# A fused attention and two-expert kernel: weight loads placed ahead of a round's chunk loads, the fourteenth weight load held back, scaled queries behind x

## The chip, the cores and the metric

The kernel runs on one core of a Trainium2 chip. The metric is the device time of one execution in microseconds (us), as the median of several runs, smaller being better. One further execution was profiled; its trace is what the rows below are read from. The engines are named as in the trace: PE (TensorE, matmuls; PEld its weight loads), DVE (VectorE), ACT (ScalarE), POOL (GpSimd) and SP (SyncE, which here issues nearly all DMAs).

## The reference

```
# decayed linear attention, per head, blocks of 64 tokens, state carried from block to block
intra = ((qb @ kb.T) * Dmask) @ vb               # Dmask[i,j] = lam**(i-j) for i >= j
inter = (qb * lam**(pos+1)) @ kv_state
out   = intra + inter
kv_state = lam**64 * kv_state + (kb * lam**(63-pos)).T @ vb
# first feed-forward, on x = attention output, 1536 tokens x 512
xn = x / sqrt(mean(x*x) + 1e-6) * rms_g
y  = (silu(xn @ w_gate) * (xn @ w_val)) @ w_out        # 512 -> 1536 -> 512
# second feed-forward
out = max(y @ w1, y @ w2, y @ w3) @ w_out2             # 512 -> 768 -> 512
```

q, k, v are float32, 2 batches x 8 heads x 768 tokens x 64. The feed-forward weights are held as 64-bit floats, which the kernel reads as pairs of 32-bit words and turns into float32 itself.

## The kernel before, in words

The 1536 tokens are 12 *chunks* of 128 tokens (two blocks of 64 each). A chunk c needs three *chunk loads*, kn, qn and vn (256 KB each, line L92, called k6, q6, v6 for chunk 6). A *weight unit* is a 128 x 512 float32 tile of one weight matrix, loaded as 512 KB of raw words (tile wraw, line L170). Units are named by matrix and index: g = w_gate, v = w_val, o = w_out, so that g0, v0, g1, v1, g2, o0, o1, v2, g3, v3, o2, o3, g4, v4 are the first fourteen loads in order (in the code they have indices 0 to 13). To keep weight unit v4 and chunk load v4 apart, the units are called "unit v4" and so on. A g or v load is three DMAs (one of 256 KB, two of 128 KB), an o load is one DMA.

Each unit is made by a chain over three engines: ACT L252 and L253 read the raw words, DVE L209, L212, L216 clamp, mask and shift, POOL L219 adds, then ACT L180 and POOL L183 split the float32 result into a high and a low float32r part (wh, wl) for three-pass matmuls on PE.

The program begins with seven hand-ordered *rounds* s = 0 to 6 of attention (a string of letters per round in `orders`, each letter a step with a lag in chunks). In round s PE does in this order: M, the output of chunk s-2 (px, L377); N, the broadcast of the norm of chunk s-3 (pb, L416); C, scores and state of chunk s-1 (sc, L321 and L326); U, the sum of squares (pm, L403); and T, the transposes of chunk s (pk L297, pq L299). After T, ACT copies kT and qT out of PSUM and DVE makes the scaled queries qs (L306) from the same PSUM bank pq. DVE's other steps in a round are x (L418, needs pb), A (L333, needs sc) and the state S (L351); from round 3 on one weight unit is put between them. `loads_at` issues the chunk loads about two chunks ahead, at the start of step T; after the round one raw unit is loaded (`load_to`).

Then comes the first feed-forward (`first_stage`): for token blocks j of 512, gate and value products pg and pv (L490), silu and product, and the output products acc (L480 to L482); the remaining attention rounds are spread between its matmuls at the *gaps* (`gap`, `spread`), and units are made at the same gaps (`third_of_unit`, which calls `begin_unit`). `begin_unit` asks for raw loads up to three units ahead of the one it begins. `lates` becomes non-empty once all attention is done. Raw tiles sit in few buffers: loads with index 10 and up share three of them, so that a load waits until POOL's L219 of the unit three loads before has read its words. SP issues all these DMAs strictly in program order, so a DMA that waits for a buffer holds back every DMA behind it.

Of the kernel before, what the change touches and what calls it, by code (L numbers as in the profile page):

```python
# [9 lines left out]
F32 = mybir.dt.float32  # L10
# [8 lines left out]
P = 128  # L19
# [7 lines left out]
def tile_decay_attention_swiglu_maxout(  # L27
# [136 lines left out]
    def load_to(n):  # L164
        while pos["load"] < min(n, len(raw_list)):
            nm, f = raw_list[pos["load"]]
            more = pos["load"] % 5 > 2 and pos["load"] < 3 * PLAIN - 2
            t = (ld if more else wp).tile([P, KD, 2 * P], I32, tag="raw", name="wraw", bufs=2 if more else 3)
            for to, src in crosswise(t, source[nm](f)) if nm in "gv" else [(t, source[nm](f))]:
                nc.sync.dma_start(out=to, in_=src)  # L170
            raws[nm, f] = t
            pos["load"] += 1
# [58 lines left out]
    def begin_unit():  # L231
        if pos["made"] == len(unit_list):
            return
        key = unit_list[pos["made"]]
        at = group_of[key] % 2
        if first_use[key] <= pos["step"] + 6 and at < len(wpools) and (key is None or room[at]):
            pos["made"] += 1
            if key is None:
                stage1.append((None,) * 5)
                return  # L240
            room[at] -= 1
            held[key] = at
            if key[0][0] == "T":
                stage1.append((key, None if second_sum(key) else words[key[0][1], key[1]], at, None, None))
                return
            load_to(pos["raw"] + (3 if pos["half"] else 1))
            pos["raw"] += 1
            t = raws.pop(key).rearrange("p k (f w) -> p (k f) w", w=2)
            lo, hi = t[:, :, 0], t[:, :, 1]
            W = wp.tile([P, 512], I32, tag="W", name="W", bufs=4)  # L250
            words[key] = W
            nc.scalar.activation(out=W.bitcast(F32), in_=hi.bitcast(F32), func=AF.Abs)  # L252
            nc.scalar.activation(out=lo, in_=lo.bitcast(U32), func=AF.Copy, scale=2.0 ** -29)  # L253
            stage1.append((key, W, at, lo, hi))
# [29 lines left out]
    def decayed_keys(c):  # L284
        keys[c] = kd = att.tile([P, H, D], F32, tag="kd", name="kd", bufs=2)
        r = slice(0, P if c % CPB != CPB - 1 else C)
        nc.gpsimd.tensor_tensor(out=kd[r], in0=qkv[c][0][r], in1=Tm[r, :, C - 1:C].to_broadcast([r.stop, H, D]),
                                op=ALU.mult)

    def turn(c):  # L290
        kn, qn, vn = qkv[c][0], qkv[c][1], qkv[c][2]
        pk = bank("pk")
        pq = bank("pq")
        pkv = pk.rearrange("p (a t) -> p a t", t=P)
        pqv = pq.rearrange("p (a t) -> p a t", t=P)
        for a in range(NP):
            nc.tensor.transpose(pkv[:, a, :], kn[:, 2 * a:2 * a + 2, :].rearrange("p h d -> p (h d)"), ident)  # L297
        for a in range(NP):
            nc.tensor.transpose(pqv[:, a, :], qn[:, 2 * a:2 * a + 2, :].rearrange("p h d -> p (h d)"), ident)  # L299
        kT = att.tile([P, NP, P], F32, tag="kT", name="kT", bufs=1)  # L300
        nc.scalar.copy(out=kT, in_=pkv)
        qT = att.tile([P, NP, P], F32, tag="qT", name="qT", bufs=1)
        nc.scalar.copy(out=qT, in_=pqv)
        qs = att.tile([P, NP, 2, C], F32, tag="qs", name="qs")
        h0 = 0 if c % CPB else 1
        nc.vector.tensor_tensor(  # L306
            out=qs[:, :, h0:], in0=pqv.rearrange("p a (h i) -> p a h i", h=2)[:, :, h0:],
            in1=lami.rearrange("p a (h i) -> p a h i", h=1).to_broadcast([P, NP, 2 - h0, C]), op=ALU.mult)
        if c == 0:
            decayed_keys(0)  # L310
        A = att.tile([P, H, C], F32, tag="A", name="A", bufs=1)
        st[c] = dict(kT=kT, qT=qT, qs=qs, vn=vn, A=A)

    def scores(c):
        d = st[c]
# [14 lines left out]
    def masked(hf):  # L330
        def piece(c):
            d = st[c]
            nc.vector.tensor_tensor(  # L333
                out=d["A"].rearrange("p (a t) i -> p t a i", t=2)[:, hf],
                in0=d["sc"][hf][:, :HF].rearrange("p (a i) -> p a i", i=C),
                in1=Tm.rearrange("p (a t) i -> p t a i", t=2)[:, hf], op=ALU.mult)
            if hf == 0:
                d["S0"] = last_state[0]
                d["S1"] = next_state(c, 0, d["S0"])
        return piece  # L340
# [82 lines left out]
    def rest(c):  # L423
# [5 lines left out]

    named = dict(M=(2, mixed), N=(3, normed), C=(1, scores), a=(1, masked(0)), R=(3, rest),  # L430
                 b=(1, masked(1)), U=(2, summed), V=(1, advance), T=(0, lambda c: (loads_at(c), turn(c))),
                 K=(-1, decayed_keys), k=(0, decayed_keys),
                 w=(3, lambda c: None))
    orders = ["MNCabUVTRK"] * (CPNB + 1) + ["MNCabUVTR", "MNCRabUkVT"] + ["MNCaUkRbVT"] * (NCH - CPNB - 2) + ["MNwRwU", "wwwNwR"]
    attn_q = [(s_, named[ch][1], s_ - named[ch][0]) for s_ in range(NCH + 3) for ch in orders[s_]
              if (ch == "K") <= s_ - named[ch][0] < NCH]
    gaps = [0, 0]
# [1 line left out]
    def attn_step():  # L439
        _, fn, c = attn_q.pop(0)  # L440
        fn(c)
# [514 lines left out]
    with tc.manual_schedule():  # L956
        nc.scalar.dma_start(out=lam8, in_=lam.rearrange("(o h) -> o h", o=1).to_broadcast([P, H]))
        loads_to(0)
        for to, src in crosswise(g_sb, rms_g.rearrange("(a p) -> p a", p=P)):
            nc.scalar.dma_start(out=to, in_=src)  # L960
        make_identity(nc, ident)
        nc.vector.memset(ones, 1.0)
        nc.vector.memset(zeros, 0.0)
        nc.scalar.activation(out=mhalf, in_=zeros[:, 0:1], func=AF.Silu)
        nc.vector.memset(mhalf, -0.5)
        warm = bank("warm")
        for i in range(9):
            nc.tensor.matmul(out=warm[:, 0:P], lhsT=zeros, rhs=zeros, start=True, stop=True)
        nc.vector.tensor_tensor(out=diag, in0=ident[:, :C], in1=ident[:, C:], op=ALU.add)
        for hf in range(2):  # L970
            nc.vector.tensor_copy(out=lamh[64 * hf:64 * hf + 64, :],
                                  in_=lam8.rearrange("p (a t) -> p t a", t=2)[64 * hf:64 * hf + 64, hf, :])
        for a in range(NP):
            nc.vector.tensor_tensor_scan(
                out=lami[:, a, :], data0=lamh[:, a:a + 1].to_broadcast([P, C]), data1=zeros[:, :C],
                initial=1.0, op0=ALU.mult, op1=ALU.add)
        for h in range(H):
            nc.vector.tensor_tensor_scan(
                out=Tm[:, h, :], data0=lam8[:, h:h + 1].to_broadcast([P, C]), data1=diag,
                initial=0.0, op0=ALU.mult, op1=ALU.add)  # L980
        loads_to(1)
        pos["narrow"] = False
        unit_ = None
        for s_ in range(CPNB + 3):
            while attn_q[0][0] == s_:
                fn = attn_q[0][1]
                attn_step()
                if s_ > 2 and fn is named["N"][1]:
                    begin_unit()
                    unit_ = stage1.pop(0)  # L990
                if unit_ and s_ == CPNB + 2:
                    if fn is named["U"][1]:
                        words_of_unit(3, *added_later)
                    elif fn is named["V"][1]:
                        for n in range(3):
                            words_of_unit(n, *unit_, split_add=True)
                        split_unit.append(unit_)
                        stage2.append(unit_[:3])
                elif unit_ and fn is named["b"][1]:
                    words_of_unit(0, *unit_)  # L1000
                elif unit_ and fn is named["U"][1]:
                    words_of_unit(1, *unit_)
                    if stage2:
                        finish_unit(*stage2.pop(0))
                elif unit_ and fn is named["V"][1]:
                    words_of_unit(2, *unit_, split_add=s_ == CPNB + 1)
                    added_later = unit_
                    stage2.append(unit_[:3])
            if s_:
                load_to(pos["load"] + 1)  # L1010
        begin_unit()
        finish = first_stage()
        pos["step"] = len(steps)
        second_stage(finish)
# [31 lines left out]
```

## Time and profile before

| | |
|---|---|
| median of 3 runs | 547.11 us (546.27 to 547.93) |
| the profiled execution's own time | 548.3 us |
| its span, first to last instruction | 546.5 us |
| PE busy | 531.0 us, 97% of the span |
| DVE, POOL, ACT busy | 371.7 us, 300.9 us, 279.7 us |
| mean granted TensorE clock | 0.993 of full speed |

The page divides the span into 40 slices; PE is at 9 tenths or more nearly everywhere except in the first seven slices, the first 95 us, where PE's share goes down to 8 and DMA's is between 7 and 8 tenths in the first five. A busy PE is not PE at its peak, since matmuls are pipelined; what counts in the sections below is where PE's sequence of matmuls stands still.

### The profile page before, as it was taken

The page shows a single profiled execution, that of the slowest core. Times are in us where ns is not written, and L with a number is a line of the kernel's source. Part 1 is how long each engine was busy: PE and PEld are TensorE (multiplying, and loading weights), DVE is VectorE, ACT ScalarE, POOL GpSimd, SP SyncE. Part 2 cuts the span into 40 slices and gives each one's busy share as a digit, 9 for nine tenths or more (in the row PEclk, how much of TensorE's full clock was granted, in tenths as well). Part 3 has the DMA queues.
Part 4 walks back from the last instruction along what each step waited for, and adds up shares of the span by engine and source line. Part 5 has one row for each costly group of instructions (what it writes and reads, how often), then busy time and mean ns, then how long its engine had stood idle before and what let it go on. Part 6 is the DMA issues. An engine that isn't in the chain of part 4 may idle for free.

```text
span 546.5 us, 9743 instructions
## 1 busy us (share of the span) xinstructions
PE 531.0 (97%) x3728; PEld 438.2 (80%) x3728; DVE 371.7 (68%) x680; ACT 279.7 (51%) x541; POOL 300.9 (55%) x247
## 2 busy tenths in 40 slices
PE   8998988999999999999999999999999999999997
PEld 7776756788888888888888888888888888888886
DVE  4776775545967676768677575887777477684464
ACT  3667674336264565464447426646466755651120
POOL 2485886241436486385556636886287544962050
PEclk9979999999999999999999999999999999999999
DMA  8888817000202132131221221121123222200015
GB/s 191 203 209 235 213 40 186 9 2 0 78 0 63 54 116 68 49 115 40 77 88 65 78 57 60 40 77 40 38 79 114 85 75 75 82 34 0 0 44 188
DMA packets 65598, 44.67 MB, mean 82 GB/s; under 512 B 40080, under 2 KB 61840, under 8 KB 65552
## 3 DMA queue, kind: packets, MB, share of 16 engines
q1 hardware_dynamic: 64848, 44.05, 28.4%
q8 instruction: 29, 0.48, 0.4%
q14 instruction: 17, 0.14, 0.1%
q10 hardware_dynamic: 704, 0.01, 0.1%
HBM read 40.90 MB, written 3.15 MB: 81 GB/s over the span
## 4 chain that ended last, share of the span: by engine, by line
PE 85%; DMA 4%; issue 2%; POOL 2%; SPq 2%; DVE 2%; ACT 2%; POOLq 0%; ACTq 0%; DVEq 0%
PE p L683 34%; PE acc L874 9%; PE r L683 8%; PE acc L480 6%; PE acc L482 6%; PE acc L481 6%; PE pv L490 5%; PE q L683 4%; PE pg L490 4%; DMA wraw<-in_moe_w_val_dram 3%; SPq L170 2%; PE px L377 1%; POOL W L219 1%; DMA qn<-in_q_dram 1%; PE sc L326 1%
## 5 line engine op out<-in xcount | busy, mean ns | idle before, releaser
L183 POOL TENSOR_TENSOR wl<-W,wh 128x512 fp32r<-128x512 f32 x77 | 100.7, 1309 | 60.5 <-ACT wh L180 60.5
L219 POOL TENSOR_TENSOR W<-W,wraw 128x512 int32<-128x512 int32 x60 | 80.6, 1343 | 71.9 <-DVE W L216 61.7
L180 ACT CAST wh<-W 128x512 fp32r<-128x512 f32 x77 | 47.8, 621 | 80.3 <-POOL W L219 78.8
L501 POOL TENSOR_TENSOR hl<-sg,hh 128x512 fp32r<-128x512 f32 x36 | 47.2, 1311 | 34.3 <-ACT hh L500 34.3
L683 PE MATMUL p<-xl,wh 128*128 128x512 f32 x148 | 57.6, 389 | 0.0
L683 PE MATMUL p<-xh,wl 128*128 128x512 f32 x148 | 57.6, 389 | 0.0
L683 PE MATMUL p<-xh,wh 128*128 128x512 f32 x148 | 57.6, 389 | 0.0
L480 PE MATMUL acc<-hh,wh 128*128 128x512 f32 x144 | 56.8, 394 | 0.7 <-DVE W L216 0.7
L481 PE MATMUL acc<-hl,wh 128*128 128x512 f32 x144 | 56.2, 390 | 0.0
L482 PE MATMUL acc<-hh,wl 128*128 128x512 f32 x144 | 56.1, 390 | 0.0
L252 ACT ACTIVATE W<-wraw 128x512 f32<-128x512 f32 x60 | 40.3, 672 | 9.9 <-DMA wraw<-in_moe_w_dram 4.4
L838 DVE TENSOR_TENSOR acc_sb<-acc,acc_sb 128x512 f32<-128x512 f32 x46 | 31.7, 690 | 19.5 <-PE acc L482 18.3
L209 DVE TENSOR_SCALAR mid<-W 128x512 f32<-128x512 f32 x58 | 39.8, 686 | 6.1 <-ACT W L252 6.1
L212 DVE TENSOR_SCALAR mid<-mid 128x512 int32<-128x512 int32 x58 | 40.3, 694 | 0.8
L216 DVE SCALAR_TENSOR_TENSOR W<-wraw,mid 128x512 int32<-128x512 int32 x58 | 39.5, 682 | 1.1
L253 ACT ACTIVATE wraw<-wraw 128x512 int32<-128x512 uint32 x60 | 39.9, 665 | 0.0
L738 ACT COPY c<-p 128x512 f32<-128x512 f32 x34 | 20.0, 587 | 38.3 <-PE p L683 38.3
L501 POOL TENSOR_TENSOR hl<-m,hh 128x512 fp32r<-128x512 f32 x18 | 24.2, 1350 | 23.0 <-ACT hh L500 23.0
L683 PE MATMUL p<-yl,wh 128*128 128x512 f32 x90 | 35.0, 389 | 0.0
L683 PE MATMUL p<-yh,wh 128*128 128x512 f32 x90 | 35.0, 389 | 0.0
L683 PE MATMUL p<-yh,wl 128*128 128x512 f32 x90 | 35.0, 389 | 0.0
L500 ACT CAST hh<-sg 128x512 fp32r<-128x512 f32 x36 | 22.3, 619 | 22.8 <-DVE sg L624 16.8
(176 smaller groups left out, 1322.9 us busy)
## 6 DMA issues: line engine op xcount, KB each, us to landing
wraw<-in_moe_w_out_dram SPq DMA_DIRECT2D x18, 512.0 KB, 3.4
wraw<-in_moe_w_dram SPq DMA_DIRECT2D x18, 512.0 KB, 3.5
kn<-in_k_dram SPq DMA_DIRECT2D x12, 256.0 KB, 4.3
qn<-in_q_dram SPq DMA_DIRECT2D x12, 256.0 KB, 4.7
vn<-in_v_dram SPq DMA_DIRECT2D x12, 256.0 KB, 4.9
wraw<-in_moe_w_gate_dram SPq DMA_DIRECT2D x12, 256.0 KB, 3.0
wraw<-in_moe_w_gate_dram SPq DMA_DIRECT2D x24, 128.0 KB, 3.3
wraw<-in_moe_w_val_dram SPq DMA_DIRECT2D x12, 256.0 KB, 3.0
```

Source lines behind the costliest of these rows:

```text
L180: nc.scalar.copy(out=wh, in_=W.bitcast(F32))
L183: nc.gpsimd.tensor_tensor(out=wl, in0=W.bitcast(F32), in1=wh.bitcast(F32), op=ALU.subtract)
L212: nc.vector.tensor_scalar(out=mid[key], in0=mid[key], scalar1=0x07FFFFFF, scalar2=3, op0=ALU.bitwise_and, op1=ALU.logical_shift_left)
L219: nc.gpsimd.tensor_tensor(out=W, in0=W, in1=lo, op=ALU.add)
L252: nc.scalar.activation(out=W.bitcast(F32), in_=hi.bitcast(F32), func=AF.Abs)
L480: nc.tensor.matmul(out=out, lhsT=wh, rhs=xh_, start=first, stop=False)
L481: nc.tensor.matmul(out=out, lhsT=wh, rhs=xl_, start=False, stop=False)
L482: nc.tensor.matmul(out=out, lhsT=wl, rhs=xh_, start=False, stop=last)
L490: nc.tensor.matmul(out=ps, lhsT=w[:, kk * P:(kk + 1) * P], rhs=x[:, kk, :], start=n == 0, stop=n == len(todo) - 1)
L501: nc.gpsimd.tensor_tensor(out=dst_l, in0=src, in1=dst_h.bitcast(F32), op=ALU.subtract)
L683: nc.tensor.matmul(out=ps, lhsT=w[:, ks], rhs=r[:, o + k, :], start=first and k == 0 and n == 0, stop=k == 1 and n == 2, skip_group_check= ...
L874: nc.tensor.matmul(out=acc[:, cs], lhsT=x[:, ts], rhs=w[:, cs], start=n == 0, stop=n == len(todo) - 1)
```

## The change

Three edits. First, in rounds 1 to 6 the raw weight load of the round is issued just ahead of step T, which starts the round's chunk loads, where it used to come after the round. Second, in the first feed-forward, as long as attention is not done, `begin_unit` asks for at most thirteen raw loads; unit v4 (index 13) is so asked for only after attention is done. Third, in rounds 0 to 5 step T (now the letter t) leaves out the scaled queries, and a new step Q makes them in the next round, behind N, whose last DVE instruction is x; the tile A is allocated where it is first written.

```diff
-            load_to(pos["raw"] + (3 if pos["half"] else 1))
+            load_to(min(pos["raw"] + 3, 3 * PLAIN + 1) if pos["half"] and not lates else pos["raw"] + (3 if lates else 1))
...
-    def turn(c):
+    def turn(c, scaled=True):
...
+        st[c] = dict(kT=kT, qT=qT, pq=pqv, vn=vn)
+        if scaled:
+            scaled_queries(c)
+        if c == 0:
+            decayed_keys(0)
+
+    def scaled_queries(c):
+        pqv = st[c].pop("pq")
         qs = att.tile([P, NP, 2, C], F32, tag="qs", name="qs")
...
-        if c == 0:
-            decayed_keys(0)
-        A = att.tile([P, H, C], F32, tag="A", name="A", bufs=1)
-        st[c] = dict(kT=kT, qT=qT, qs=qs, vn=vn, A=A)
+        st[c]["qs"] = qs
...
+            if hf == 0:
+                d["A"] = att.tile([P, H, C], F32, tag="A", name="A", bufs=1)
...
+                 t=(0, lambda c: (loads_at(c), turn(c, False))), Q=(1, scaled_queries),
...
-    orders = ["MNCabUVTRK"] * (CPNB + 1) + ["MNCabUVTR", "MNCRabUkVT"] + ["MNCaUkRbVT"] * (NCH - CPNB - 2) + ["MNwRwU", "wwwNwR"]
+    orders = ["MNQCabUVtRK"] * (CPNB + 1) + ["MNQCabUVtR", "MNQCRabUkVT"] + ["MNCaUkRbVT"] * (NCH - CPNB - 2) + ["MNwRwU", "wwwNwR"]
...
+                if s_ and fn in (named["t"][1], named["T"][1]):
+                    load_to(pos["load"] + 1)
                 attn_step()
...
-            if s_:
-                load_to(pos["load"] + 1)
```

The first place is SP's queue around the end of the rounds. The piece is a difference: the rows above it end with unit v1, and vn, kn, qn in its first lines are v5, k6 and q6.

```order
 L170 DMA wraw<-in_moe_w_val_dram 64x2x256 x2
 L92 DMA vn<-in_v_dram 128x8x64
+L92 DMA kn<-in_k_dram 128x8x64
+L92 DMA qn<-in_q_dram 128x8x64
 L170 DMA wraw<-in_moe_w_gate_dram 128x2x256
 L170 DMA wraw<-in_moe_w_gate_dram 64x2x256 x2
+L92 DMA vn<-in_v_dram 128x8x64
+L170 DMA wraw<-in_moe_w_out_dram 128x1024
 L92 DMA kn<-in_k_dram 128x8x64
 L92 DMA qn<-in_q_dram 128x8x64
 L92 DMA vn<-in_v_dram 128x8x64
```

Before, unit v1 stood behind v5, k6 and q6 and was followed by v6; now it stands ahead of these three, unit g2 ahead of v6, and unit o0 ahead of the loads of chunk 7. In every round from 1 on, the three chunk loads and the unit have changed places in this way.

The second place is SP's queue at the last two chunks. In this piece of the difference the gate rows are unit g4, the removed rows are unit v4, and kn and qn are those of chunk 10.

```order
 L170 DMA wraw<-in_moe_w_gate_dram 128x2x256
 L170 DMA wraw<-in_moe_w_gate_dram 64x2x256 x2
-L170 DMA wraw<-in_moe_w_val_dram 128x2x256
-L170 DMA wraw<-in_moe_w_val_dram 64x2x256 x2
 L92 DMA kn<-in_k_dram 128x8x64
 L92 DMA qn<-in_q_dram 128x8x64
```

Unit v4's three DMAs now follow the six loads of chunks 10 and 11.

The third place is DVE in rounds 4 to 5: before, and then of the changed kernel (its line numbers are shifted; L314 is qs, L425 is x).

```order
L216 SCALAR_TENSOR_TENSOR W<-wraw,mid 128x512
L306 TENSOR_TENSOR qs<-pq,lami 128x512
L418 TENSOR_TENSOR x<-x,pb 128x512
L333 TENSOR_TENSOR A<-sc_680,Tm 128x4x64
```

The changed kernel has at the same place, after the same row of W:

```order
L425 TENSOR_TENSOR x<-x,pb 128x512
L314 TENSOR_TENSOR qs<-pq,lami 128x512
```

The two change places in rounds 2 to 5's boundaries (four times); on PE, ACT and POOL every instruction stands where it stood.

## Rows read from the trace of the kernel before

**Rows 1.** Windows by stage: busy time by engine, granted clock, DMA share, GB/s.
```profile
0.00:39.30 39.30, 34.51 (x793) 30.74 (x794) 27.45 (x95) 23.02 (x56) 19.12 (x24) 0.91 0.85 202
39.30:92.30 53.00, 45.76 (x661) 34.73 (x660) 37.02 (x85) 35.87 (x77) 39.95 (x36) 1.00 0.63 164
...
120.00:527.00 407.00, 407.00 (x1797) 337.18 (x1797) 284.19 (x456) 209.81 (x380) 229.31 (x177) 1.00 0.19 59
```

**Rows 2.** Waits of PE, 14 to 100 us: total us, times, longest.
```profile
PE pk L297 <- DMA kn<-in_k_dram: 1.5, 1, 1.5
...
PE pm L403 <- DVE zeros L394: 1.2, 3, 0.6
PE px L377 <- ACT sg L621: 1.1, 1, 1.1
PE pb L416 <- DVE mid L212: 1.1, 1, 1.1
```

**Rows 3.** Timeline of PE at the transposes of chunk 10: start, us, idle before.
```profile
87.62 0.39 PE L490 MATMUL pg<-xh,wl 128*128 128x512 f32 x1
89.50 0.63 PE L297 MATMUL pk<-ident,kn 128*128 128x128 f32 x4 [1.49 <-DMA kn<-in_k_dram]
90.45 0.41 PE L299 MATMUL pq<-ident,qn 128*128 128x128 f32 x2 [0.33 <-DMA qn<-in_q_dram]
```

**Rows 4.** Timeline of SP, 64 to 92 us: units g4 and v4, then k10.
```profile
69.09 1.69 SPq L170 DMA_DIRECT2D wraw<-in_moe_w_gate_dram  x3
84.16 1.67 SPq L170 DMA_DIRECT2D wraw<-in_moe_w_val_dram  x3
85.92 0.54 SPq L92 DMA_DIRECT2D kn<-in_k_dram  x1
```

**Rows 5.** The chain that ended last, 60 to 120 us: start, us, what.
```profile
82.82 1.32 POOL W L219
```

**Rows 6.** Timeline of SP, 26 to 47 us: q6, then unit v1.
```profile
29.75 1.79 SPq L92 DMA_DIRECT2D qn<-in_q_dram  x1
31.59 4.04 SPq L170 DMA_DIRECT2D wraw<-in_moe_w_val_dram  x3
```

**Rows 7.** The chain, 0 to 60 us: last DMA of unit v1, issue to landing.
```profile
35.03 4.89 DMA wraw<-in_moe_w_val_dram
```

**Rows 8.** DMA issues at 29.9 us (q6 alone): count, size, us from issue to landing.
```profile
qn<-in_q_dram SPq DMA_DIRECT2D x1, 256.0 KB, 6.4
```

**Rows 9.** Timeline of PE where the rounds end and the first feed-forward begins.
```profile
39.02 0.60 PE L299 MATMUL pq<-ident,qn 128*128 128x128 f32 x4
39.38 0.48 PE L490 MATMUL pg<-xh,wh 128*128 128x512 f32 x1
```

**Rows 10.** Waits of ACT, 14 to 52 us: total us, times, longest.
```profile
ACT W L252 <- DMA wraw<-in_moe_w_val_dram: 3.2, 2, 2.2
...
ACT W L252 <- DMA wraw<-in_moe_w_gate_dram: 1.6, 2, 1.2
ACT W L252 <- DMA wraw<-in_moe_w_out_dram: 0.7, 1, 0.7
```

**Rows 11.** Waits of DVE, 0 to 39.5 us: total us, times, longest.
```profile
DVE A L333 <- PE sc L326: 4.4, 4, 1.6
...
DVE x L418 <- PE pb L416: 1.2, 2, 0.8
...
DVE qs L306 <- ACT qT L303: 0.3, 1, 0.3
```

**Rows 12.** Windows of 5 us, columns as in rows 1.
```profile
25.00:30.00 5.00, 3.66 (x135) 2.94 (x133) 4.04 (x13) 4.02 (x12) 4.02 (x5) 1.00 0.80 203
30.00:35.00 5.00, 4.89 (x72) 4.38 (x76) 4.98 (x17) 3.64 (x8) 5.00 (x6) 0.53 0.77 174
35.00:40.00 5.00, 5.00 (x89) 4.43 (x81) 2.79 (x9) 2.19 (x7) 2.92 (x4) 0.79 0.87 237
```

**Rows 13.** Timeline of PE, 43.5 to 51.3 us: two stops in the first feed-forward.
```profile
45.60 0.35 PE L403 MATMUL pm<-ones,zeros 128*128 128x1 f32 x2 [0.61 <-DVE zeros L394]
...
51.12 0.28 PE L377 MATMUL px<-qs,S 64*64 64x64 f32 x3 [1.14 <-ACT sg L621]
```

## The prediction

> **What bounds the kernel now.** I read the windows by stage first, to see where PE can gain at all. From 120 to 527 us PE is busy for all of the 407.00 us; from 39.3 to 92.3 us it is busy for 45.76 of 53.00, so some 7 us stand still there; before 39.3 us it is busy for 34.51, partly at half clock [rows 1]. PE's work and its order are the same in both kernels. From about 92 us on the kernel is PE-bound; what PE gains or loses before that goes to the end one for one. The reader is to see that the 97% of the page hides the one stretch that matters.
>
> The list of PE's waits, read next, names what makes PE stand: the longest single one is pk waiting for kn, 1.5 us, then three single ones of about 1.1 us that end in other engines [rows 2]. The timeline says where: at the transposes of chunk 10 PE stops 1.49 us for kn and 0.33 us for qn [rows 3].
>
> **Why k10 is late.** On SP, unit g4's loads are issued at 69.09, unit v4's at 84.16, and k10 at 85.92, right behind them [rows 4]. Unit v4's buffer comes free when POOL's L219 ends, 82.82 + 1.32 = 84.14 [rows 5], and 84.16 is that end: for 15 us SP stands at unit v4, and k10, with a buffer of its own, stands behind it. k10 then reaches PE 89.50 - 85.92 = 3.6 us after its issue.
>
> **Part 1, unit v4 held back.** Its three DMAs go behind the loads of chunks 10 and 11, so k10 can be issued once unit g4's are, 69.09 + 1.69 = 70.8. With the 3.6 us above it is there at about 75, 14 us before it is wanted. Both waits at chunk 10 go: 1.49 + 0.33 = 1.82 us. The lower bound is 0 (another wait takes the place). For the upper, the step from pg's 0.39 us at 87.62 to pk at 89.50 was 1.88, of which 0.39 is work [rows 3]; with qn's wait nothing beyond 1.9 can be there; 2.1 if the small gaps go too. I take **-1.8**. Unit v4 itself is asked for after attention; it was issued at 84.16 before and its place in unit order is unchanged, and everything behind 92 us ran without a PE stop, so its lateness I cost at 0; if that cover were gone its landing would cost a few tenths, which I put into the range.
>
> **Part 2, unit loads ahead of the chunk loads, rounds 1 to 6.** In a round the unit load gains three chunk loads and each chunk load loses a unit load. In the case I can price best, unit v1 stood behind q6: q6 issued at 29.75 for 1.79 us, unit v1 for 4.04 us from 31.59 [rows 6], its last part landing at 35.03 + 4.89 = 39.92 [rows 7]. Alone, q6 took 6.4 us from 29.9, so it landed at 36.2 or so [rows 8]. SP issues back to back, and the three loads that follow are the same bytes in another order. What stood last of this group now stands first: unit v1 lands early, q6 takes the last place, 39.92. PE's pq, the transposes of q6, began at 39.02 and pg, the first matmul of the first feed-forward, at 39.38 [rows 9]. If pq now waits for 39.92 to 40.0, that stage starts **+1.0** later. Bounds: the DMA engines moved 203, 174 and 237 GB/s in three stretches of 5 us around here [rows 12]; at 237 throughout, the bytes of 25 to 39.9 (203 x 5 + 174 x 5 + 237 x 4.9 = 3046 KB) would take 12.9 us in place of 14.9, so q6 would be there at 37.9, before 39.02, and pq would start when the chain ahead of it allows. That chain was itself waiting for units, so it may be earlier by up to 1.1: -1.1. The other end is +1.5, q6 half a us behind the forecast. I take +1.0, since the order of the bytes is certain and a better rate is not.
>
> What the units gain is on ACT: from 14 to 52 us its W read waits 3.2 us for v units, 1.6 for g units and 0.7 for an o unit [rows 10]. Each such wait delays ACT's queue (the copies kT and qT, sg and g1) and DVE's mid behind it. Two of PE's stops in the first feed-forward follow from it: pm waits 0.61 at 45.60 and px 1.14 at 51.12, behind DVE's zeros and ACT's sg [rows 13]. With units there about 4 us sooner, the sum of 1.75 is the upper bound, 0 the lower; I take **-1.7**, because both stand right behind a unit's late arrival and nothing else late is in sight. The 1.1 us that pb waits for mid at about 27 us [rows 2] goes too, but it only lets the rounds run sooner to the next late chunk load, so I count 0 for it.
>
> **Part 3, scaled queries behind x.** On DVE the two change places four times. DVE waited at x for pb 1.2 us in two rounds, at qs 0.3 us once for ACT's qT, and at A, the next instruction, 4.4 us in four rounds for PE's scores [rows 11]. If DVE stands at pb, qs is now later by that wait; if not, x is sooner by one instruction. qs is read by px, a round later, and x by pm, behind the scores; the 4.4 us, 1.1 in each of the four rounds, hide a shift of either. If that cover were gone, the 0.3 us of qs in each of four rounds, 1.2 us, would be lost, or x's 1.2 us gained. I take **0**, with bounds of 1.2 either way.
>
> **Sum.** -1.8 + 1.0 - 1.7 + 0 = -2.5 us. The sum is made against the profiled execution's own 548.3 us (span 546.5), which becomes 545.8; that execution is 1.2 above the median of the runs, 547.11, so the forecast for the median is **544.6**. What a measurement of this kernel can tell from no change is about 0.3%, 1.64 us: faster is below 545.47, slower above 548.75.
>
> **Rivals.**
>
> *B, the loads run ahead.* With SP's queue never behind a unit's buffer, q6 lands at 37.9 and nothing is paid at 39; the other gains stand: -1.8 - 1.7 - 1.1 = -4.6, so 542.5. For it speaks that the rate did reach 237 GB/s late in the rounds; against it that at 25 to 35 us nothing but the queue held it at 174 to 203 and the order of the bytes does not change that.
>
> *C, the clock falls as the stage begins.* The granted clock was 1.00 from 25 to 30 us, where PE was busy for 3.66 of 5 us, then 0.53 and 0.79 in the next two windows [rows 12]: after the stop at about 27 us the 2.4 GHz level gave way to 1.2 GHz for a time, and 5 x 0.47 + 5 x 0.21 = 3.4 us of full-speed time were lost, mostly hidden by the wait for loads. If PE now waits for q6 near 39, the half-speed stretch can come behind it, in the first feed-forward, where every matmul is on the path: 3.4 us not or half absorbed give -2.5 + 1.7 to 3.4, so 546.3 to 548. Against it: the wait is 1 us, and the clock did not fall after the stops of 0.61, 1.14 and 1.49 us later on (1.00 from 39.3 to 92.3 us [rows 1]); for it, that the stop that preceded the fall was no longer than these. The Trainium skill, "TensorE: Matmul & The Clock Gate", section "HAM oscillation — how this bites in real kernels", says that a kernel whose bursts of matmuls are parted by waits for DMAs drops back to the lower clock each time and starts the next burst slow. By that rule the rounds, which are such bursts, would stay slow as long as loads are late, and the result would be about 548.0; the trace agrees in the rounds, and not from 39.3 us on.
>
> *D, only chunk 10 gains.* ACT, DVE and POOL are so near their limit between 39.3 and 92.3 us (DVE 37.02, ACT 35.87, POOL 39.95 of 53 us [rows 1]) that units that land sooner only wait for them; -1.8 + 1.0 stays: 546.3.
>
> *E, slower.* The chunk loads are what PE waits for in the rounds, and each is now behind a unit. If this holds from round to round, the rounds end later by a unit's place in the queue, 4.04 us [rows 6], in place of 1.0. With chunk 10's gain whole and ACT's halved the sum is 4.0 - 1.8 - 0.9 = +1.3, 548.4; the longer wait makes a fall of the clock as in C likely, 1.7 to 3.4 more, so 550.1 to 551.8. With the smaller of these it is slower by over 1.64 us from where the first feed-forward begins 1.64 + 2.7 - 1.7 = 2.6 us later, at 42.0. For it speaks that loads are the bound to 39 us; against it, that the bytes ahead of q6 are the same ones in both orders.
>
> **How the numbers follow.** Chances: the forecast, 543.0 to 545.4, 0.43; B 0.13; C 0.22; D 0.10; E 0.12. Faster is the forecast and B, 0.56; same is C and D, 0.32; slower is E, 0.12. The likeliest case alone has 543.0 to 545.4 (the bounds of its terms: chunk 10's 0 to -2.1, the stage's start -1.1 to +1.5, ACT's 0 to -1.75, not all at one end). The range reaches down to B less part 3's bound, 542.5 - 1.2, some 541.5, and up to the end of C, 548.2; it leaves out E and the ends of the others, under 2 in 10.
>
> **What the profile after would show.** Part 1: k10's issue near 71 us and no idle ahead of pk at chunk 10; unit v4 issued behind chunk 11's loads, without a PE wait. Part 2: unit v1 landing near 35 and q6 near 40 us; pq with an idle time before it that qn's DMA ends; pg starting near 40.3; ACT's waits for units under 1 us in 14 to 52 us; no stop of PE at pm and px. Part 3: DVE's A wait and x's wait as before within 1 us. The prediction is wrong if pg starts before 38.5 (B) or after 42.0 (E), if the granted clock from 39.3 us on is under 0.98 (C), or if the two stops in the first feed-forward stay (D) or unit v4's load brings a new one behind 92 us.

## The result, and the profile after

| | before | changed |
|---|---|---|
| first series, median | 546.78 us (4 runs, 546.27 to 547.93) | 542.07 us (4 runs, 541.52 to 543.4) |
| ratio, first series | | 0.9914, 95% interval 0.9889 to 0.994 |
| ratio, a later series (8 runs of the changed kernel) | | 0.9936, 95% interval 0.9912 to 0.996 |
| profiled execution, time and span | 548.3 and 546.5 us | 542.33 and 540.5 us |

The change is faster: 4.7 us in the first series, 3.5 us by the ratio of the later one. The forecast was 2.5 us, 544.6 us, with a range from 541.5 to 548.2. The two profiled executions lie 6.0 us apart, more than the medians, and that difference needs explaining too.

The windows of the changed kernel answer to [rows 1] and [rows 12]; the columns are the same (PE, PEld, DVE, ACT, POOL, granted clock, DMA share, GB/s).

```profile
0.00:39.30 39.30, 33.20 (x835) 28.70 (x839) 29.45 (x99) 25.64 (x61) 21.82 (x27) 1.00 0.90 216
39.30:92.30 53.00, 48.97 (x738) 37.97 (x742) 36.95 (x83) 35.34 (x80) 40.34 (x36) 1.00 0.66 171
...
25.00:30.00 5.00, 4.68 (x143) 3.92 (x142) 5.00 (x16) 4.75 (x13) 5.00 (x6) 1.00 0.87 202
30.00:35.00 5.00, 4.53 (x128) 3.87 (x126) 4.84 (x14) 3.79 (x11) 4.46 (x5) 1.00 0.95 222
35.00:40.00 5.00, 3.73 (x81) 2.91 (x81) 3.53 (x10) 3.63 (x8) 4.08 (x4) 1.00 0.91 265
```

Two things are to be seen. From 39.3 to 92.3 us PE is busy for 48.97 us where it was 45.76, and gets through 738 matmuls of the trace where it got through 661. And the granted clock is 1.00 from 25 to 40 us, where before it had gone down to 0.53 and 0.79; the loads run at 222 and 265 GB/s there, where they ran at 174 and 237.

The timeline of PE in the changed kernel, at the places of [rows 9], [rows 13] and [rows 3] (the last two rows are chunk 10's transposes):

```profile
35.33 0.63 PE L297 MATMUL pk<-ident,kn 128*128 128x128 f32 x4
37.12 0.63 PE L299 MATMUL pq<-ident,qn 128*128 128x128 f32 x4 [1.16 <-DMA qn<-in_q_dram]
37.50 0.48 PE L498 MATMUL pg<-xh,wh 128*128 128x512 f32 x1
...
42.82 0.28 PE L410 MATMUL pm<-ones,zeros 128*128 128x1 f32 x2
...
47.42 0.28 PE L384 MATMUL px<-qs,S 64*64 64x64 f32 x3 [0.32 <-ACT sg L629]
...
84.15 0.60 PE L297 MATMUL pk<-ident,kn 128*128 128x128 f32 x4
84.59 0.60 PE L299 MATMUL pq<-ident,qn 128*128 128x128 f32 x4
```

The forecast's wait is there: pq stands 1.16 us for chunk 6's queries, which now come behind unit v1. But pk ahead of it starts at 35.33 us in place of 38.55, so the first feed-forward begins 1.88 us earlier, at 37.50, in spite of the wait. The stop at pm is gone, that at px is 0.32 in place of 1.14 us, and chunk 10's transposes follow without a wait. On SP, k10 now goes right behind unit g4, and unit v4 (wraw from w_val, the last row) behind chunk 11's loads, as its timeline shows:

```profile
65.37 1.69 SPq L170 DMA_DIRECT2D wraw<-in_moe_w_gate_dram  x3
67.16 0.54 SPq L92 DMA_DIRECT2D kn<-in_k_dram  x1
...
72.33 0.80 SPq L92 DMA_DIRECT2D vn<-in_v_dram  x1
80.45 1.68 SPq L170 DMA_DIRECT2D wraw<-in_moe_w_val_dram  x3
```

### The profile page after: what moved, and what is told of

It reads as the page before. It is cut to its first block, busy times and chain, and to the rows that moved or that the text cites. A ratio compares the mean times of both kernels' runs of the same rounds, so it can differ in the third digit from the quotient of the medians.

```text
span 540.5 us, 9748 instructions
## 1 busy us (share of the span) xinstructions
PE 527.1 (98%) x3728; PEld 434.8 (80%) x3728; DVE 371.1 (69%) x680; ACT 279.5 (52%) x541; POOL 300.8 (56%) x247
## 3 DMA queue, kind: packets, MB, share of 16 engines
q1 hardware_dynamic: 64848, 44.05, 28.5%
## 4 chain that ended last, share of the span: by engine, by line
PE 89%; POOL 3%; issue 3%; ACT 1%; DMA 1%; DVE 1%; SPq 0%; POOLq 0%; ACTq 0%
PE p L691 34%; PE acc L882 9%; PE r L691 9%; PE acc L488 6%; PE acc L489 6%; PE acc L490 6%; PE pv L498 5%; PE pg L498 5%; PE q L691 4%; PE px L384 2%; POOL W L219 1%; PE pm L410 1%; PE sc L326 1%; PE sc L331 1%; PE pk L297 1%
## 5 line engine op out<-in xcount | busy, mean ns | idle before, releaser
L219 POOL TENSOR_TENSOR W<-W,wraw 128x512 int32<-128x512 int32 x60 | 80.6, 1343 | 71.6 <-DVE W L216 66.8
L216 DVE SCALAR_TENSOR_TENSOR W<-wraw,mid 128x512 int32<-128x512 int32 x58 | 39.5, 681 | 1.1
```

The lines of the kernel that those rows point to most:

```text
L219: nc.gpsimd.tensor_tensor(out=W, in0=W, in1=lo, op=ALU.add)
```

## The experiments

The theory before these runs (theory U) put the whole gain down to units that land sooner and to unit v4; the rival (theory Q) put the gain in the rounds down to the third edit. Twelve runs were made in three series; a gain in us below is worked out from the ratio, which goes by all executions, and the difference of the medians is given where it reads differently. The diffs of single edits are against the kernel before, the others against the changed kernel. (Where an edit is left out, the tile A still is allocated where it is first written, except with unit v4 held back alone.)

**Units ahead alone (first edit).** The kernel before, with the two places of `load_to` changed:

```diff
+                if s_ and fn in (named["t"][1], named["T"][1]):
+                    load_to(pos["load"] + 1)
                 attn_step()
...
-            if s_:
-                load_to(pos["load"] + 1)
```

> The unit loads of rounds 1 to 6 ahead of the chunk loads, nothing else changed. Theory U (units that land sooner take away the wait of pb for mid, the fall of the clock behind it, and the two stops in the first feed-forward): 3.7 of the 5.9 us by which the profiles differ, so the median 3 to 3.7 us below before; first pg of the feed-forward near 37.5 us, clock 1.00 throughout, chunk 10's waits of some 2 us still there. Theory Q (the scaled queries behind x free DVE for x and the clamp, and it is this that keeps the rounds moving): at most 1.5 us below before, with a PE stop at pb of round 5 as before.

Measured: 544.16 us, ratio 0.9985 (0.9965 to 1.0006), 0.8 us; 1.5 us by the medians. Two of its twelve executions, at 547.34 and 548.39 us, make that difference. pg started at 35.50 us, the clock was 1.00, no stop was left at pb of round 5 or at the pm of [rows 13], and at chunk 10 PE stopped 1.31 and 0.59 us. But px stopped 1.15 us as before. Theory U missed the size and one of the two stops; the time alone would meet theory Q's mark, the missing stop at pb does not. Against the kernel before the edit is not clear of the noise.

**Unit v4 held back alone (second edit).**

```diff
-            load_to(pos["raw"] + (3 if pos["half"] else 1))
+            load_to(min(pos["raw"] + 3, 3 * PLAIN + 1) if pos["half"] and not lates else pos["raw"] + (3 if lates else 1))
```

> Unit v4 held back until attention is done, nothing else changed. Both theories: the two waits at chunk 10 go and nothing else moves, 1.8 to 2.2 us below before. The rival that another wait takes the place: within 0.5 us of before, with a new stop of PE between 84 and 100 us, or at unit v4's first use.

Measured: 543.69 us, ratio 0.9966 (0.9953 to 0.998), 1.9 us, as expected. The timeline of PE in this kernel, which has the rounds of the kernel before unchanged:

```profile
26.99 0.49 PE L416 MATMUL pb<-ident,diag 128*128 128x128 f32 x2 [0.49 <-DVE mid L212]
...
48.59 0.28 PE L377 MATMUL px<-qs,S 64*64 64x64 f32 x3 [1.17 <-ACT sg L621]
...
85.34 0.60 PE L297 MATMUL pk<-ident,kn 128*128 128x128 f32 x4
85.77 0.60 PE L299 MATMUL pq<-ident,qn 128*128 128x128 f32 x4
```

Chunk 10's waits are gone. The surprise stands in the first row: pb of round 5 waits 0.49 us and starts at 26.99, where in the profile of before it waited 1.11 and started at 28.14, with the same order of every load and instruction up to there. So the early part of that first profile was not what this order always does.

**Scaled queries behind x alone (third edit).** The kernel before with `scaled_queries`, t and Q as in the change, and both other edits left out.

> The scaled queries behind x, nothing else changed. Theory U: within 0.5 us of before, since DVE waits at A for scores in these rounds whichever of the two comes first. Theory Q: 1.5 to 3 us below before, with the first pg of the feed-forward before 38 us.

Measured: 545.22 us, ratio 0.9991 (0.9969 to 1.0013). pg started at 35.55 us, which by itself would meet theory Q's mark, but the kernel with only unit v4 held back, whose queries stand where they were, has pg at 35.91. No difference can be measured.

**The change without its third edit.**

```diff
-    orders = ["MNQCabUVtRK"] * (CPNB + 1) + ["MNQCabUVtR", "MNQCRabUkVT"]
+    orders = ["MNCabUVTRK"] * (CPNB + 1) + ["MNCabUVTR", "MNCRabUkVT"]
```

> The change without its third edit: units ahead, unit v4 held back, scaled queries where they were. Theory U: as fast as the change, within 0.5 us. Theory Q: 1.5 to 3 us slower than the change.

Measured: 541.98 us, ratio 0.9929 (0.9909 to 0.9948), as the change. Theory Q has fallen. This kernel also differs from the one with unit v4 held back alone by the first edit alone (and by where A is allocated), and the two ran in the same series: 541.98 against 543.69 us, with ratios whose intervals do not touch (0.9909 to 0.9948, 0.9953 to 0.998). So the first edit is worth 1.7 us by the medians and 2.0 us by the ratios where unit v4 is held back.

**The change without its first edit.** The unit's `load_to` back behind the round.

> The change without its first edit: unit loads behind the chunk loads as before, unit v4 held back, scaled queries behind x. Theory U: 1.8 to 2.2 us below before, the rounds and the stops at pm and px as before. Theory Q: 3.5 us or more below before.

Measured: 543.45 us, ratio 0.9944 (0.9919 to 0.997), 3.1 us, which is above theory U's 1.8 to 2.2 us and below theory Q's 3.5; the interval, some 1.6 to 4.4 us, holds both. The stops at pm and px did not come "as before" either: none at pm, and 0.33 us at px. In its profiled execution the clock fell in the rounds. Windows of 2 us, same columns:

```profile
18.00:20.00 2.00, 1.48 (x19) 1.41 (x20) 1.08 (x5) 1.22 (x3) 0.00 (x0) 1.00 0.66 151
20.00:22.00 2.00, 1.89 (x41) 1.54 (x39) 2.00 (x7) 1.49 (x3) 0.55 (x1) 0.67 0.96 262
22.00:24.00 2.00, 2.00 (x42) 1.66 (x46) 1.24 (x5) 0.74 (x3) 0.73 (x1) 0.50 0.56 145
...
30.00:32.00 2.00, 1.89 (x68) 1.52 (x66) 0.18 (x2) 0.52 (x3) 1.90 (x2) 0.77 0.82 188
32.00:34.00 2.00, 2.00 (x74) 1.93 (x64) 2.00 (x7) 2.00 (x7) 1.64 (x2) 1.00 0.92 251
```

Some 10 us at half clock made pg start at 39.42, as late as in the first profile of before, but chunk 6's queries and unit v1 had landed at about 33 and 35 us. So a late start of the stage does not need late loads.

**Units ahead in rounds 1 to 3 only.**

```diff
-                if s_ and fn in (named["t"][1], named["T"][1]):
+                if s_ and s_ < 4 and fn in (named["t"][1], named["T"][1]):
...
+            if s_ and not (s_ < 4):
+                load_to(pos["load"] + 1)
```

> The change with the unit loads ahead in rounds 1 to 3 only; in rounds 4 to 6 they stand behind the chunk loads as before. If the gain in the rounds comes from units v0 and g1 being there in time (no stop at pb, no fall of the clock), the first pg of the feed-forward starts as early as in the change or earlier, 36.0 to 37.5 us, for chunk 6's queries no longer stand behind unit v1; the stops at pm and px in the first feed-forward return in part, 0 to 1.8 us. Sum 1.5 us faster to 1.5 us slower than the change. If the gain comes from unit v1 and those behind it, the start is near 39.4 as before and the kernel 2 us or more slower than the change.

Measured: 543.1 us, ratio 0.9936 (0.991 to 0.9961). pg at 36.59, clock 1.00, and the stops at pm (0.35 us) and px (1.15 us) are there, as expected; the one at px was there with all units ahead too (1.15 us, first edit alone), so it does not tell the two orders apart.

**Units ahead in rounds 4 to 6 only.** The same diff with `s_ > 3`.

> The change with the unit loads ahead in rounds 4 to 6 only; in rounds 1 to 3 they stand behind as before. If units v0 and g1 make the gain in the rounds, PE stops about 1 us at pb of round 5 again, the clock falls behind it, and the first pg starts at 39 us or later; with unit v1 ahead of chunk 6's queries it may be 40, as the prediction had it: 2 to 3.5 us slower than the change. If units v1 and later make the gain: within 0.7 us of the change.

Measured: 542.42 us, ratio 0.9922 (0.9893 to 0.9951). The profile shows what was expected, one round later: a stop at pb, and the clock falling behind it.

```profile
33.59 0.49 PE L423 MATMUL pb<-ident,diag 128*128 128x128 f32 x2 [1.69 <-DVE mid L212]
...
38.92 0.78 PE L498 MATMUL pg<-xh,wh 128*128 128x512 f32 x1
```

In the windows of 2 us from 34 us on the clock is 0.72, 0.50, 0.50 and 0.58. The median does not show it: this execution took 544.87 us, the median is 542.42. Of the six executions this one and one of 544.09 us have a mean granted clock of 0.994 or less, the other four 0.997 and 541.44 to 542.93 us. The fall belongs to some executions, not to all.

**Round 4's unit (unit v1) behind, the others ahead.** The same diff with `s_ != 4`.

> The change, but in round 4 alone the unit load (unit v1) stands behind v5, k6 and q6 as before. PE's wait of 1.16 us for q6 at the last transposes of the rounds goes, and the first pg starts near 36.2 us. If unit v1, then some 4 us later, is still in time for ACT, the kernel is about 1.2 us faster than the change; if ACT waits for it, the stops in the first feed-forward return and it is within 0.5 us of it or up to 1 us slower.

Measured: 542.14 us, ratio 0.9922 (0.9893 to 0.9952). The wait for chunk 6's queries is gone and pg starts at 35.06; px waits 0.99 us for ACT's sg. No difference from the change can be measured. That wait at px is not the price of unit v1's place, for the change itself has 1.00 us there in its second profile, below.

**The kernel before, a second time.**

> The kernel before once more, for a second profile of it. If the first profile of before shows what it does in most executions, PE stops about 1 us at pb of round 5, the clock falls to half behind it and the first pg starts near 39.4 us again. If that execution was one of the slower ones (what the runs with the same loads, with only unit v4 held back and with only the scaled queries moved, suggest: pg at 35.9 and 35.6, clock 1.00 to 40 us), pg starts at 35.5 to 36.5 us, the stops at pm and px are 0.5 to 1.2 us, chunk 10's waits 1.5 to 2 us, and the span is near 543.5 us.

Measured: 545.67 us, ratio 0.9996 (0.9976 to 1.0015). The second expectation holds but for chunk 10's waits, which are longer: pg at 35.73 us, and the timeline of PE, at the places of [rows 13] and [rows 3] and at pb of round 5, reads

```profile
26.94 0.49 PE L416 MATMUL pb<-ident,diag 128*128 128x128 f32 x2 [0.34 <-DVE mid L212]
...
47.33 0.28 PE L377 MATMUL px<-qs,S 64*64 64x64 f32 x3 [1.16 <-ACT sg L621]
...
85.62 0.63 PE L297 MATMUL pk<-ident,kn 128*128 128x128 f32 x4 [1.43 <-DMA kn<-in_k_dram]
87.19 0.63 PE L299 MATMUL pq<-ident,qn 128*128 128x128 f32 x4 [0.94 <-DMA qn<-in_q_dram]
```

Its windows of 5 us answer to [rows 12]:

```profile
25.00:30.00 5.00, 4.43 (x144) 3.84 (x143) 4.80 (x14) 4.52 (x12) 4.76 (x6) 1.00 0.97 246
30.00:35.00 5.00, 4.63 (x129) 4.00 (x128) 5.00 (x16) 4.53 (x13) 4.91 (x5) 1.00 0.94 235
```

The same loads in the same order ran at 235 GB/s from 30 to 35 us where the first profile had 174, and unit v1 landed at 31.75 + 3.6 = 35.4 us, not at 39.92.

**The change, a second time.**

> The change once more, for a second profile and more times. Both readings: the first pg starts at 36.5 to 37.5 us with a wait for chunk 6's queries ahead of it, no wait at chunk 10, 542 us as before. By the reading that the profile of before was a slow execution the difference of the medians in this series is 3 to 4 us; by the reading that it was a usual one, 4.5 us or more.

Measured: 542.19 us, ratio 0.9936 (0.9912 to 0.996), 3.5 us: the first reading; by the medians it is 4.0, between the two. The start of pg, which both readings put behind a wait for chunk 6's queries, did not come so. Chunk 6's queries, issued at 30.17 us and landing 4.5 us later, at 34.7, are in time for pq, as the timeline of PE shows:

```profile
34.92 0.63 PE L297 MATMUL pk<-ident,kn 128*128 128x128 f32 x4
35.39 0.60 PE L299 MATMUL pq<-ident,qn 128*128 128x128 f32 x4
35.74 0.48 PE L498 MATMUL pg<-xh,wh 128*128 128x512 f32 x1
...
46.43 0.28 PE L384 MATMUL px<-qs,S 64*64 64x64 f32 x3 [1.00 <-ACT sg L629]
```

So the wait for them, 1.16 us in the first profile, comes and goes with the landing; pg starts at the same time in both kernels, 35.73 and 35.74 us. The stop at px, 0.32 us in the first profile of the change, is 1.00 us here.

**Units ahead in rounds 5 and 6 only.** The same diff with `s_ > 4`.

> The change with the unit loads ahead of the chunk loads in rounds 5 and 6 only (units g2 and o0); units g0, v0, g1 and v1 behind as before. If unit v1's landing is what ACT and POOL wait for at the start of the first feed-forward, most of the first edit's gain is gone: pb of chunk 5 near 50.6 us as with all units behind, and 0.8 to 1.5 us slower than the change. If units g2 and o0 make it, pb of chunk 5 comes at 48.5 to 49.4 us and the kernel is as fast as the change or up to 1 us faster, since chunk 6's queries are not held back.

Measured: 543.59 us, ratio 0.9947 (0.9927 to 0.9967), 1.4 us slower than the change by the medians of one series, though the intervals overlap. pb of chunk 5 came at 52.31 us, outside both marks, with the clock at 0.64, 0.50, 0.50 and 0.65 in the windows of 2 us from 34 to 42 us; the execution does not separate unit v1 from units g2 and o0.

**Round 4's unit behind, and no third edit.** The diffs of round 4's unit behind and of the change without its third edit, together.

> The change with round 4's unit load (unit v1) behind its chunk loads and without the third edit (scaled queries where they were). If the third edit is worth nothing, as fast as the same kernel with it, within 0.5 us; if it is worth something, 1 us or more slower. If holding chunk 6's queries back costs what the wait at pq shows, 0.5 to 1 us faster than the change in the same series.

Measured: 542.61 us, ratio 0.9931 (0.9906 to 0.9957): as fast as the change, again without a measurable worth of the third edit or of chunk 6's queries. No version beats the change.

## Why the prediction was right, and which of its steps did not hold

Direction, range and the term of unit v4 held; the forecast had between half and seven tenths of the gain. In part that was luck. The measured 542.07 us lies outside the likeliest case of 543.0 to 545.4; it is inside the range only because that was drawn down for rival B. And the one term that was to cost time, +1.0, did not. The terms, read from the timelines of PE in two pairs of profiles (start of pg; from there to pm of chunk 8; from there to px of chunk 9; times before less after):

| term | forecast | first pair | second pair |
|---|---|---|---|
| start of the first feed-forward | +1.0 | 37.50 - 39.38 = -1.88 | 35.74 - 35.73 = +0.01 |
| stops between it and chunk 8 | -1.7 | 43.00 - 44.82 = -1.82 | 43.78 - 44.65 = -0.87 |
| chunk 10's transposes | -1.8 | 8.03 - 10.26 = -2.23 | 8.04 - 10.81 = -2.77 |
| rest to the end | 0 | -0.02 | +0.06 |
| sum, as the spans differ | -2.5 | -5.95 | -3.57 |

*Part 1, unit v4.* Right in mechanism, and shown by the run with this edit alone. The stretch from pm of chunk 8 to px of chunk 9 takes 8.03 or 8.04 us in all ten profiles with unit v4 held back, and 10.08 to 10.81 us in the four without it. The term was 0.4 us short of even its own profile, for it added the two idle times and left out the slower steps around them; from one execution to the next the waits differ by another half us. Unit v4's lateness cost nothing, as forecast, but not because something covered it: there was none. Its buffer comes free at the same place in the work, so it is issued 0.05 and 0.03 us ahead of pm of chunk 8 in the two profiles of the change (80.45 and 79.49 us) and 0.04 and 0.06 us ahead of it before (84.16 and 80.32). What moved is only the six chunk loads, out from behind it. SP itself stood for 13.4 us there, from the end of unit g4's issue at 70.78; the prediction's 15 us count from its start.

*Part 2, units ahead.* The first step that failed is the start, forecast +1.0 and measured -1.88 and 0.01: q6 was taken to land at 39.92 us, where unit v1's last part had landed, and the stop at pb and the fall of the clock behind it were counted at 0, as hidden by the wait for that load. The rule of the same bytes in another order held: in the second pair unit v1 lands at 35.4 before, and q6, in its place, at 34.7 after. But the time did not hold from one execution to the next: 39.92 and 35.4 us for unit v1 in two executions of the same kernel. Nor was the stretch hidden: with pb's wait and the half clock gone, pk of chunk 6 came 3.2 us sooner in the first pair, and the q6 wait, though as long as forecast (1.16 against 1.0), took back only a part. The stops behind the start shrank by the 1.8 us forecast in the first pair and by half of it in the second. ACT's wait for g, v and o units in 14 to 52 us went from 5.5 us [rows 10] and 3.0 in the two profiles of before to 0.3 and 0.9 in those of the change.

The second step that failed is to price the start and the stops at pm and px as terms of their own. The stop at px was put down to a unit's late arrival; but with ACT hardly waiting for units it is still 1.00 us in the change's second profile and 1.15 with units ahead alone, and without the first edit it was 0.33. What releases it is sg, which stands on ACT behind a wh that waits for POOL's L219. These are the rows of that L219 in the timelines of POOL: first profile of before and of the change, then the second ones.

```profile
48.60 1.31 POOL L219 TENSOR_TENSOR W<-W,wraw 128x512 int32<-128x512 int32 x1
44.92 1.30 POOL L219 TENSOR_TENSOR W<-W,wraw 128x512 int32<-128x512 int32 x1
44.81 1.31 POOL L219 TENSOR_TENSOR W<-W,wraw 128x512 int32<-128x512 int32 x1
43.91 1.31 POOL L219 TENSOR_TENSOR W<-W,wraw 128x512 int32<-128x512 int32 x1
```

In all fourteen profiles this px starts 2.50 to 2.52 us after that L219, and pm of chunk 8 then 33.05 to 33.10 us after this px, whenever pg started (35.06 to 39.65 us) and however long PE stopped. So the stretch has one term, the time of that L219: 3.68 us sooner in the first pair and 0.90 in the second, which is the sum of the first two rows of the table within 0.04 us. That L219 came 7.42 us after pg at the least (the change's first profile) and 10.17 at the most (unit v4 held back alone). Where the units lag, PE stands at px for what it had gained at pg: in the change's second profile pg is 1.76 us sooner than in the first, L219 only 1.01.

One reading of the rows was wrong without consequence: of the "three single ones of about 1.1 us" [rows 2], pm's 1.2 us are three waits, the longest 0.6, and a single wait of 1.4 us, of sc for ACT's x, is not among them; it is still 1.46 us in the change.

*Part 3.* Right: with it or without it no difference could be measured in three comparisons.

*The rivals.* B gave 542.5, next to the measured 542.07, and by the prediction's own sign, pg before 38.5 us, it is B that came, in both profiles (37.50 and 35.74). Its condition, loads that run ahead of the byte count of before, is what the traces show, though in the first profile a wait was paid all the same; but the order of the loads is not shown to be the reason, since the kernel before has the better rate too in its second profile. C did not come in the profiles: the clock was 1.00 throughout in both of the change. The section "HAM oscillation — how this bites in real kernels" of the Trainium skill's "TensorE: Matmul & The Clock Gate", on which the prediction drew for C, describes a kernel whose bursts of matmuls are shorter than the waits for DMAs between them. The change had no such wait: before the 1.16 us for q6 PE had been busy for 4.53 of the 5 us from 30 us on, and no fall followed. Neither D's nor E's time came; D's sign, stops that stay, did for the stop at px in the second profile.

**The first profile of before.** How far it was unusual can be read from all fourteen profiles. The clock fell within the rounds in four of the seven with the units of rounds 1 to 3 behind (the first of before, the change without its first edit, rounds 4 to 6 only, rounds 5 and 6 only), in none of the seven with them ahead; the fall in the second profile of before, and one with the scaled queries moved alone, came later, in the first feed-forward. In those four pm of chunk 8 came at 82.47 to 84.20 us; in the other three with units behind, at 80.38, 80.58 and 81.69; with all six rounds' units ahead, at 79.52 to 80.50. By these single profiles the first edit gives some 0.9 us where the clock stays up (the mean of the three, 80.88, against 80.01 of the four), and 2.5 to 4.2 us against that mean where it would have fallen.

The mean granted clock, measured in every execution of the three series, profiled or not, says more. The four falls in the rounds gave 0.991 to 0.994. At 0.994 or less are 23 of 79 executions of the kernel before, 12 of 49 of the other kernels with the units of rounds 1 to 3 behind, and 3 of 49 with them ahead. So falls of that size are rarer with the units ahead, but they come: two of the three are those of the first edit alone at 547.34 and 548.39 us. That the units' place prevents a fall is argued from these counts; no kernel forced one. Nor is the fall the main part of the gain. Among executions with a mean clock of 1.000 in the first series of experiments, the first edit takes the mean from 544.90 (9 of before) to 543.66 us (5), and with unit v4 held back from 543.45 (4) to 541.47 (4): 1.2 and 2.0 us.

Two things stay open. One is why the same loads ran at 174 GB/s in one execution and at 235 in another. The other is which unit's place carries the gain. Unit v1's does not: with round 4's unit alone behind, that L219 comes at 44.05 and 44.16 us (with and without the third edit), as early as in the change. With units v1, g2 and o0 behind it came at 46.19, but there unit v1 ended ACT's wait at 37.87 us and not at 35.88, behind the same loads, so a chance landing can be the reason as well.

## What to carry to other kernels

A DMA that waits for a buffer can hold up everything behind it on its queue, as unit v4 held k10: look for a long gap between two issues and at what stands behind it, and move the loads that need not wait out from behind it. Price a reordering of loads from more than one profile of the kernel before: here one landing differed by 4.5 us between two executions, and with it the start of a stage. Before stops of an engine are added up, look for one step that releases the last of them; if it sets the time, the stops and the start before them are not terms of their own. Moving a step on an engine that then waits for something else anyway gained nothing here.

## What the runs showed of the hardware

The granted clock fell from 1.00 to 0.50, from the 2.4 to the 1.2 GHz level, for some 3 to 10 us after stops of PE of 1.07 us (18.5 us, change without its first edit), 1.11 (first profile of before), 1.69 (rounds 4 to 6 only), 0.58 (rounds 5 and 6 only, at pb) and 1.16 (at px, second profile of before and scaled queries alone). It did not fall after equal ones: 1.16 us at q6 in the change, 1.15 and 1.17 at px with units ahead alone and with unit v4 held back alone. The length of one stop does not decide. The Trainium skill, "TensorE: Matmul & The Clock Gate", section "What's actually happening", says that the chip's observation of PE runs freely and is not reset when a kernel starts, and gives this as why the place where the clock changes differs from run to run. The traces agree that it differs: in the two profiles of the kernel before the clock first fell in the windows that begin at 30 and at 48 us. No run here shows the reason.

A fall need not cost what the clock says. In the second profile of before it came in the first feed-forward:

```profile
46.00:48.00 2.00, 0.74 (x25) 0.47 (x24) 0.54 (x1) 1.84 (x4) 1.27 (x2) 1.00 0.66 180
48.00:50.00 2.00, 2.00 (x30) 1.70 (x30) 0.60 (x1) 1.37 (x3) 2.00 (x4) 0.73 0.78 225
50.00:52.00 2.00, 2.00 (x25) 1.25 (x27) 0.70 (x2) 1.05 (x3) 2.00 (x2) 0.50 1.06 239
52.00:54.00 2.00, 2.00 (x61) 1.75 (x54) 1.84 (x3) 1.16 (x5) 1.48 (x3) 0.92 1.01 274
```

That is 2 x (0.27 + 0.50 + 0.08) = 1.7 us of full-speed time. Yet from the end of px's stop to pb of chunk 6 this kernel took 61.97 - 47.33 = 14.64 us, and with unit v4 held back alone, where the clock stayed up, 63.03 - 48.59 = 14.44: 0.2 us, which is gone again at pm of chunk 8 (33.05 against 33.10 us after px). The fall with the scaled queries moved alone, in the same place, does the same (14.64 and 33.10). In this stretch PE stops for other engines, so that its slower matmuls had room; that they filled these stops is the likely reason, not shown by itself.
